# Unread matmuls in the last attention layer: extending the filler rule of a four-layer attention kernel to its final layer

## The chip, the cores and the metric

The kernel runs on one core of a Trainium2 chip. The core has a matrix engine (TensorE, PE in the profile; its weight loads are shown apart as PEld), a vector engine (VectorE, DVE), a scalar engine (ScalarE, ACT), a general engine (GpSimd, POOL) and a queue engine that issues transfers (SyncE, SP). Matmul results land in PSUM, a memory of 8 banks of 512 float columns by 128 partitions. The metric is the device time of one execution in microseconds (us), taken as the median of several runs. The profile also reports the share of its full clock that TensorE was granted, in 3.4 us steps; in this trace it is always 1.00 or 0.50.

## The reference

Four attention layers act on x of 2048 rows by 640. Each is x = x + attention(layernorm(x)) @ wo, with 32 heads of 20 columns. Layers 0 and 2 look back over a window of 256 rows; layers 1 and 3 let every query see every key (there is no causal mask).

```python
qkv = (x @ wqkv).reshape(B, S, 3, H, Dh)           # H = 32, Dh = 20
scores = einsum("bhqd,bhkd->bhqk", q, k) * Dh ** -0.5
# layers 0 and 2 only: scores = where(0 <= i - j < 256, scores, -1e9)
p = softmax(scores)
o = einsum("bhqk,bhkd->bhqd", p, v)
x = x + o.reshape(B, S, D) @ wo
```

## The kernel before

**Units, banks and tiles.** The work is cut into units (layer l, chunk c of 512 query rows, group g of four heads). A unit has one bank of scores for each pair of key block (128 keys) and head: a matmul with 32 rows (20 used) and 512 columns, four heads in four row groups of the array. Banks are handled in tiles of three, sometimes four: the score matmuls of a tile (L1308) fill PSUM banks 0 to 2 (even tiles) or 3 to 6 (odd tiles), one ACT instruction takes the exponential of the whole tile to SBUF (L1339), and some tiles later the value matmuls (L1373) multiply it with the values, which carry a column of ones, so that each head gives 21 rows. These sum up in bank 7. Scores of tile t wait until ACT has read tile t-2.

**Order.** The order of instructions on each engine is written out by the program as it runs through the tiles. Per tile: the owed unread matmuls (L1302, see below), the scores, the exponential, then `pump` (a budget of other work), `keep_clock`, value matmuls of an earlier tile, a step of the side work on VectorE, and masks for windowed layers. Other work is held in generators (tasks) that yield what they cost: layernorm, projections (L364, L465), output projections (L552, `t_out`; L584 for a part of the last one), and tails (`t_tail`), which scale a finished unit by its sums: four or eight tiny matmuls with `sel4` (L1043), a reciprocal (L1048), a transpose (L1060), a copy (L1064), four matmuls with `spread4` (L1081), a product (L1085). From layer 1 on, tasks have a single bank, number 6, for their results (`take_m`, `drop_m`), which an odd four-bank tile also uses.

**The final layer.** Its units with c = 0 are woven into earlier work. Units (3,1,0) to (3,3,7) follow with no other unit between them, from about 1611 us on; `index[3, 1, 0, None]` is the first one's place. The tasks in this stretch are the tails, the output projections of layer 3 and the part of the last one. In these units the last key block of all four heads is not given to ACT: VectorE computes its exponential by a polynomial (L910 to L941, from scores made by L903 in bank 6), and L1382 multiplies it with the values.

**Unread matmuls.** A matmul of the identity with a mask, 128 rows by 128 columns by 512, is put in where TensorE has little to do; nothing reads its result. `state["heat"]` counts full-size matmuls of a tile, `state["least"]` says how many a tile should have, `state["carry"]` brings over a surplus of at most 3, and `state["floor"]` is a least for each tile by itself. While a tile has too few (`cool`), `keep_clock` first advances a task that may run, and otherwise emits an unread matmul: by `unread` (L634) to bank 6 if that is free, or as one owed (L1302), which goes to the first bank of the next tile, ahead of its scores. `warm_bank` does the same in tails. With `least` at 0.0 none of these emit anything. `fill` (L1030) emits a fixed number in the tail of the very last unit.

## Time and profile before

| | us |
|---|---|
| median of 8 runs | 2284.76 (2281.76 to 2287.79) |
| the profiled execution | 2288.22 |
| its span, first to last instruction | 2286.5 |
| PE busy | 1982.6 (87%) |
| ACT busy | 2170.3 (95%) |
| DVE busy | 1271.8 (56%) |
| POOL busy | 271.0 (12%) |
| mean granted TensorE clock | 0.861 |

The profile page gives busy time by engine, and the span in 40 slices of 57 us, in which a digit is the busy share in tenths (9 is 90% or more) and the row PEclk is the granted clock in tenths. Other views are answers of the trace for a stretch of time: busy times by stretch, the waits of an engine with what ended them (total us, times, longest us), and the timeline, whose lines give start, duration, engine, line, result and operands, a count, and in brackets the idle time before and what ended it. The durations of matmuls are modelled and overlap; the time from one start to the next is what a matmul takes of the engine. An ACT row can begin before the one ahead has ended.

### The profile page before, as it was taken

How to read it: one execution, taken by the hardware profiler on the slowest of the kernel's cores; microseconds unless marked ns; L12 is line 12 of the kernel's file. 1: busy time of each engine (PE TensorE's matmuls, PEld its weight loads, DVE VectorE, ACT ScalarE, POOL GpSimd, SP SyncE). 2: the span in 40 equal slices, each digit the busy share in tenths (PEclk: the TensorE clock that was granted, in tenths of full speed). 3: DMA queues.
4: the chain of work that ended last, by engine and by line, in shares of the span. 5: the costliest groups of instructions: out<-in, count | busy, mean ns of one | idle time of the engine just before them, and what ended most of it. 6: DMA issues, size and time to landing. Idle time of an engine off the chain costs nothing.

```text
span 2286.5 us, 40030 instructions
## 1 busy us (share of the span) xinstructions
PE 1982.6 (87%) x15586; PEld 705.4 (31%) x15746; DVE 1271.8 (56%) x2214; ACT 2170.3 (95%) x1741; POOL 271.0 (12%) x445
## 2 busy tenths in 40 slices
PE   8899999989898998888888988898878888888887
PEld 3333343333233333233332333232221122112222
DVE  6767675435454566455564644432565565666662
ACT  7789899999999989999899999999999999999997
POOL 4322313201100122001210022011000000000000
PEclk9999999999999999999999999999755565556556
DMA  6223222322210233002320043112111111111100
GB/s 193 79 75 98 81 80 89 97 75 58 67 33 14 60 93 97 14 27 62 100 75 14 16 116 95 28 43 72 57 47 30 30 39 33 30 38 41 36 17 15
DMA packets 88284, 135.16 MB, mean 59 GB/s; under 512 B 20766, under 2 KB 63486, under 8 KB 88094
## 3 DMA queue, kind: packets, MB, share of 16 engines
q1 hardware_dynamic: 68878, 79.43, 12.6%
q0 software_dynamic: 19216, 53.17, 7.8%
q8 instruction: 123, 2.02, 0.4%
q14 instruction: 67, 0.55, 0.1%
HBM read 99.52 MB, written 27.79 MB: 56 GB/s over the span
## 4 chain that ended last, share of the span: by engine, by line
ACT 45%; PE 29%; issue 16%; DVE 9%; DMA 0%; SPq 0%; ACTq 0%; POOL 0%; DVEq 0%; POOLq 0%
ACT pt L1339 43%; PE ps L1308 7%; PE ps L364 6%; PE ps L552 5%; PE ps L1373 4%; PE ps L465 3%; DVE pt L1410 2%; PE ps L634 2%; DVE st L314 1%; DVE on L1085 1%; ACT ka L1339 1%; PE ps L1081 1%; DVE x_sb L561 1%; PE ps L429 0%; DVE raw_o L910 0%
## 5 line engine op out<-in xcount | busy, mean ns | idle before, releaser
L1339 ACT ACTIVATE pt<-ps 128x1536 bf16<-128x1536 f32 (+2 forms) x1638 | 2096.6, 1478 | 78.7 <-PE ps L1308 69.7
L1308 PE MATMUL ps<-qt,kt 32*128 32x512 bf16 x4008 | 637.6, 453 | 176.3 <-ACT pt L1339 143.2
L1373 PE MATMUL ps<-pt,vt 128*21 128x512 bf16 x3852 | 463.2, 452 | 7.1 <-issue 4.5
L1308 PEld LDWEIGHTS <-kt 32*128 32x128 bf16 x4008 | 186.2, 94 | 594.4 <-issue 575.5
L1410 DVE TENSOR_TENSOR pt<-pt,masks 128x1024 bf16<-128x1024 bf16 (+6 forms) x403 | 209.3, 553 | 151.1 <-ACT pt L1339 150.7
L634 PE MATMUL ps<-masks,ident 128*128 128x512 bf16 x708 | 244.4, 388 | 27.9 <-DVE on L1085 7.1
L364 PE MATMUL ps<-xnT,wqk 128*128 128x512 bf16 x761 | 208.2, 385 | 19.1 <-DVE on L1085 3.9
L1373 PEld LDWEIGHTS <-vt 128*21 128x21 bf16 x3960 | 99.9, 90 | 339.0 <-issue 326.8
L314 DVE CAST st<-ps 128x512 bf16<-128x512 f32 x134 | 92.6, 691 | 187.1 <-PE ps L364 177.1
L552 PE MATMUL ps<-wop,on 128*128 128x320 bf16 x928 | 163.4, 314 | 8.3 <-DVE x_sb L561 5.2
L910 DVE TENSOR_SCALAR xnT<-ps 128x512 int32<-128x512 f32 x88 | 60.8, 691 | 186.3 <-PE ps L903 186.3
L1308 PE MATMUL ps<-qa,ka 32*128 32x384 bf16 (+2 forms) x1408 | 118.5, 278 | 28.0 <-ACT pt L1339 22.6
L1085 DVE TENSOR_TENSOR on<-on,ps 128x512 bf16<-128x512 bf16 x128 | 86.3, 684 | 65.8 <-PE ps L1081 64.7
L561 DVE TENSOR_TENSOR x_sb<-x_sb,ps 128x320 bf16<-128x320 bf16 x120 | 58.0, 483 | 113.0 <-PE ps L552 112.9
L857 DVE CAST on<-ps 128x512 bf16<-128x512 f32 x112 | 77.1, 688 | 74.9 <-PE ps L1373 48.0
L465 PE MATMUL ps<-wv,xnT 128*128 128x320 bf16 x640 | 111.7, 303 | 7.9 <-DVE on L1085 3.1
L552 PEld LDWEIGHTS <-on 128*128 128x128 bf16 x928 | 83.4, 101 | 76.2 <-issue 47.6
L364 PEld LDWEIGHTS <-wqk 128*128 128x128 bf16 x830 | 70.2, 98 | 112.0 <-issue 55.7
L634 PEld LDWEIGHTS <-ident 128*128 128x128 bf16 x798 | 59.8, 97 | 132.7 <-issue 131.4
L398 POOL TENSOR_SCALAR rstd<-mv 128x4 f32<-128x4 f32 x15 | 4.1, 277 | 774.4 <-DVE mv L385 753.6
L1373 PE MATMUL ps<-pt,va 128*21 128x384 bf16 (+2 forms) x1408 | 76.2, 284 | 3.9 <-DVE pt L1410 1.6
L1308 PEld LDWEIGHTS <-ka 32*128 32x128 bf16 x1408 | 43.2, 92 | 96.3 <-issue 86.4
(101 smaller groups left out, 1585.1 us busy)
## 6 DMA issues: line engine op xcount, KB each, us to landing
vt<-v_d SPq DMA_DIRECT2D x48, 336.0 KB
kt<-k_d SPq DMA_DIRECT2D x192, 80.0 KB
wqk<-in_B_wqkv_dram POOLq DMA_DIRECT2D x80, 160.0 KB, 3.6
wqk<-in_A_wqkv_dram POOLq DMA_DIRECT2D x70, 160.0 KB, 3.4
k_d<-st POOLq DMA_DIRECT2D x75, 128.0 KB, 2.2
q_d<-st POOLq DMA_DIRECT2D x75, 128.0 KB, 2.2
qt<-q_d SPq DMA_DIRECT2D x384, 20.0 KB
v_d<-vs POOLq DMA_DIRECT2D x16, 336.0 KB, 3.0
```

The source lines that it names most:

```text
L314: nc.vector.tensor_copy(out=out_, in_=in_)
L364: nc.tensor.matmul(pq, lhsT=wt[:, dc, :], rhs=xt[:, dc, :], start=(dc == 0), stop=(dc == KD - 1),)
L465: nc.tensor.matmul(pv, lhsT=xt[:, dc, i * P : (i + 1) * P], rhs=wv_sb[l % 2][:, dc, h * HD : (h + 1) * HD], start=(dc == 0), stop=(dc == K ...
L552: nc.tensor.matmul(yp, lhsT=on[:, g, qb * P : (qb + 1) * P], rhs=wop[:, g, i * HD : (i + 1) * HD], start=(g == a), stop=(g == b - 1),)
L561: nc.vector.tensor_tensor(out=xv, in0=had, in1=yp, op=ALU.add)
L634: nc.tensor.matmul(ps[:, b, :], lhsT=ident[:], rhs=masks[:, 0, :], start=True, stop=True)
L857: nc.vector.tensor_copy(out=oT, in_=op)
L1085: nc.vector.tensor_tensor(out=oT, in0=oT, in1=zb, op=ALU.mult)
L1308: nc.tensor.matmul(sp[:, i, col * P : (col + qn) * P], lhsT=u.k(kc, j), rhs=u.q(j, q0, qn), start=True, stop=True,)
L1339: nc.scalar.activation(out=pt[:, i:k, b0 * P :], in_=sp[:, i:k, b0 * P :], func=ACT.Exp, scale=SCALE,)
L1373: nc.tensor.matmul(op[32 * j : 32 * j + VW, q0 * P : (q0 + qn) * P], lhsT=u.v(kc, j), rhs=pg[:, i, col * P : (col + qn) * P], start=(first ...
L1410: nc.vector.tensor_tensor(out=pt_[:, i:k, cols], in0=pt_[:, i:k, cols], in1=mv_, op=ALU.mult)
```

## The change

In the kernel before, `least` is 0.0 from unit (3,1,0) on. In the changed kernel it is 1.76 for a three-bank tile (2.35 for a four-bank one) there too, as in the units before; `floor` was 0.9 already. So `keep_clock` and `warm_bank` act in the final layer as they do in layers 1 and 2: they emit unread matmuls, and `keep_clock` may advance tasks. No other line differs.

```diff
                 for i, b in enumerate(cur):
                     pts.append((t, pt, i, b))
-                warmth = 1.76 if state["unit"] >= woven else 1.0
-                state["least"] = warmth * n_b / 3 if state["unit"] < index[3, 1, 0, None] else 0.0
+                state["least"] = (1.76 if state["unit"] >= woven else 1.0) * n_b / 3
                 state["floor"] = 0.9 if state["unit"] >= index[1, 1, 0, None] else 0.0
```

## The prediction

> **What bounds the kernel now.** I read the forty slices first, because they show stages. The last ten slices (from about 1611 us on) are the final layer.

> ```profile
> PE   8899999989898998888888988898878888888887
> ACT  7789899999999989999899999999999999999997
> PEclk9999999999999999999999999999755565556556
> ```

> No stage but this one runs at about half the TensorE clock, though TensorE counts as busy there, and ScalarE (ACT, the exponentials) is at 9 all the way. Next come busy times by stretch: a stretch of layers 1 and 2 with unread matmuls in it, the final layer to its last exponential, and two short stretches of half clock in earlier layers.

> ```profile
> core 0: us, PE busy (x) PEld busy (x) DVE busy (x) ACT busy (x) POOL busy (x), PEclk, DMA share, GB/s
> 600.00:800.00 200.00, 178.87 (x1449) 65.74 (x1465) 105.88 (x192) 198.14 (x172) 9.04 (x13) 1.00 0.13 35
> ...
> 1611.00:2273.00 662.00, 545.19 (x3456) 145.90 (x3456) 386.60 (x485) 649.22 (x474) 0.00 (x0) 0.55 0.11 33
> ...
> 580.00:583.40 3.40, 2.96 (x11) 0.64 (x11) 1.19 (x2) 2.90 (x2) 0.00 (x0) 0.50 0.20 50
> ...
> 842.80:846.20 3.40, 3.40 (x13) 0.79 (x12) 0.56 (x2) 1.81 (x2) 0.00 (x0) 0.50 0.28 84
> ```

> In the final layer ACT is busy 649.2 of 662 us: it is the bound, and all that a faster TensorE can give back before the last exponential is the missing 12.8 us. ACT's own waits in that stretch say who owns them:

> ```profile
> ACT pt L1339 <- PE ps L1308: 10.8, 15, 1.6
> ACT pt L1339 <- PE ps L903: 1.7, 1, 1.7
> ```

> That is 12.5 us in 16 waits, all for scores. The timeline shows what such a wait looks like at half clock:

> ```profile
> 1649.70 2.31 PE L552 MATMUL ps<-wop,on 128*128 128x320 bf16 x8
> 1651.94 0.61 PE L1373 MATMUL ps<-pt,vt 128*21 128x512 bf16 x4
> ...
> 1652.48 0.61 PE L1308 MATMUL ps<-qt,kt 32*128 32x512 bf16 x3
> ...
> 1653.20 2.79 ACT L1339 ACTIVATE pt<-ps 128x1536 bf16<-128x1536 f32 x2 [1.41 <-PE ps L1308]
> ```

> Eight output matmuls take 2.24 us from start to the next start, so the next scores come 1.41 us late. At full clock the same group takes 1.19 us (1638.32 to 1639.51). Between output projections ACT runs one three-bank tile every 1.345 us at either clock (75 tiles in 100.85 us at 1.00 from 1400 on; score matmuls 1.34 us apart at 0.50 from 1722.71 on), so there the clock buys nothing.

> **The change part by part.** Compared instruction by instruction, the program gains 747 matmuls of 128x512, each with its weight load: 303 by L634 (798 to 1101) and 444 by L1302 (70 to 514, in 268 groups of one to three, ahead of a tile's scores). All stand from the first tile of unit (3,1,0) on. Tasks move by a tile or so (output matmuls now also go 2+6), three more four-bank tiles appear for four three-bank ones, and ACT's elements and POOL's queue stay as they are. On SP one output write of c = 0 (L567) now stands ahead of the nine loads of one unit (L771 to L785) instead of behind them. It waits for its output matmuls, and the loads behind it: at most from 1644.6, where they were issued, to about 1658, the end of the fourth group of eight. A unit of 60 banks lasts 60/3 x 1.345 = 27 us and the loads are issued at the end of a unit's scores with one more unit loaded, so I cost this at nothing; without that cover it would be up to 13 us.

> *Does it hold the clock?* From 600 to 800 us there were 158 + 16 unread matmuls, and 112 + 25 real ones of 320 columns and 20 of 128; in units of 128x512 that is 174 + 86 + 5 = 265 per 200 us, at 1.00. The final layer gets 747 + 148 x 0.625 + 32 x 0.6 = 859 in 662 us, 259 per 200 us. So nearly the same, and I take 1.00. [...] The row says 0.55 at 82% busy, so it is the size of the matmuls (32 rows for scores, 21 columns for values) that fails to hold it here, and I go by the row.

> *What the fillers cost TensorE.* Start-to-start at full clock, from the stretch after 1400 us:

> ```profile
> 1421.33 0.40 PE L1308 MATMUL ps<-qt,kt 32*128 32x512 bf16 x3
> 1421.66 0.39 PE L634 MATMUL ps<-masks,ident 128*128 128x512 bf16 x1
> 1421.98 0.40 PE L1373 MATMUL ps<-pt,vt 128*21 128x512 bf16 x4
> 1422.67 0.39 PE L1308 MATMUL ps<-qt,kt 32*128 32x512 bf16 x3 [0.30 <-ACT pt L1339]
> ...
> 1424.02 0.38 PE L1302 MATMUL ps<-masks,ident 128*128 128x512 bf16 x1
> ...
> 1426.14 0.59 PE L634 MATMUL ps<-masks,ident 128*128 128x512 bf16 x2 [0.39 <-DVE on L1085]
> 1426.66 0.40 PE L1373 MATMUL ps<-pt,vt 128*21 128x512 bf16 x4
> ```

> Scores 0.33, a first unread matmul 0.32, two 0.52, values 0.33; L1302 takes 0.31 before its scores (1424.33). A usual tile (two unread, scores, values) is 0.52 + 0.33 + 0.33 = 1.18 us, under ACT's 1.345. For the whole stretch: 478 score groups x 0.33, 370 value groups x 0.33, 747 fillers x 0.27 (half first, half second) = 202, output matmuls 148 x 0.15 + 32 x 0.16, 88 side matmuls x 0.28, fourteen tails x 1.1: 158 + 122 + 202 + 27 + 25 + 15 = 549 of 662 us, 83%. It fits on the average.

> *Tile by tile* it is tight. Two L1302 in front start 0.05 after ACT frees the banks, scores follow at 0.57, ACT can start 0.50 after the scores' start (2242.76 to 2243.26), so at 1.07; ACT's own pace asks for about 1.25. Spare: 0.18 us. Three in front (six times) are 0.04 late: 0.3 us in all. A pair of tiles with a side matmul (L903) needs 1.46 + 1.18 = 2.64 of 2.69. Two tiles of a tail with fillers (0.33 + 0.32 + 0.32 + 0.33, then 0.31 more) need 2.91 of 2.69, and a filler on bank 6 waits for VectorE to read it, as at 1426.14 (0.39 us); behind that filler stand the values and the next scores, and ACT waits for these. Some 0.2 us for each of 14 tails is 3 us, and output matmuls of c = 0 (1.19 + 0.66 against 1.345) lose 1 to 2. From both sides: nothing if the slack takes it all, and 12 us if each of the 28 scalings stalls by 0.39. Nearest row: 600 to 800 us has fillers, side work, tails and outputs together and leaves ACT idle 200 - 198.14 = 1.86 us; times 662/200 it is 6.2 us. I take 6.2.

> *Dips of the clock* remain: with fillers on, the two stretches above fell to 0.50 for one window of 3.4 us and came back. ACT's waits around them sum to 0.17 + 0.35 + 0.97 = 1.5 and 0.36 + 0.59 + 1.60 = 2.6 us. None occurs from 850 to 1611 us. I take half of one, 1 us; bounds 0 and 5 dips (10 us).

> *After the last exponential* (2273.8 to 2286.5):

> ```profile
> 2275.34 1.44 PE L1030 MATMUL ps<-masks,ident 128*128 128x512 bf16 x3
> ...
> 2276.71 0.29 PE L1060 MATMUL ps<-ident,hl 128*32 128x128 bf16 x1
> ```

> Three fillers at half clock hold the transpose to 2276.71, though its operand was written by 2276.26. At full clock they take 0.32 + 2 x 0.21 = 0.74 (1.37 now), with one more by warm_bank 0.95: the transpose starts 0.4 earlier, the one filler after it saves 0.2, four L1081 0.54 to 0.32 another 0.2, the next three fillers 0.4. With the last values 0.1 to 0.2: -1.3 us. Bounds: 0 and -2.

> **Sum**, against the profiled execution's span 2286.5: -12.5 + 6.2 + 1.0 - 1.3 = -6.6, span 2279.9. That run took 2288.22, 3.5 over the median of eight, so from the median 2284.76 - 6.6 = 2278.2 us. [...]

> **Rivals.** Measurement tells 0.2% (4.6 us) from no change.
> 1. *TensorE's order becomes the wait* (slower side). Place: fillers ahead of scores (268 groups) and ahead of tails. For it: 0.18 us of spare and 2.91 against 2.69. Against: 600 to 800 us. It decides once it costs ACT over 12.5 + 1.3 + 4.6 = 18.4 us, 69 ns for each of the 268 groups, that is if a tile's matmuls take some 10% more than above. At 8 to 12%, with 14 to 20 us of new waits, 2285 to 2291.
> 2. *The clock dips often.* Tail tiles carry one filler instead of two. Each dip 1.5 to 2.6 us: six to twelve give 2284 to 2301. Against: none in 750 us before the final layer.
> 3. *The clock is not held at all*, and 747 fillers at 0.43 to 0.60 us come to 388 on top of 545: 933 against 662, +270 us, about 2555. Against: nearly equal filler rates.
> 4. *Nothing moves:* the output projections' waits stay because VectorE's reading of bank 6 paces them, or old and new waits cancel: 2281 to 2288. Against: the waits vanish at full clock (four of L584 per tile after 2243.3 leave no ACT wait).

> **How the numbers follow.** Forecast 0.55 (own range 2271 to 2282: all waits gone at one end, five us more at the other); of it 0.48 is faster by more than 0.2%, 0.07 within. Rival 1 0.20 (0.08 within, 0.12 slower), rival 2 0.15 (0.01 and 0.14), rival 3 0.04 slower, rival 4 0.06 within. Faster 0.48, same 0.22, slower 0.30. The range 2270 to 2293 leaves out rival 3, half of rival 2 and a little at either end.

> **What would show it.** Right: slices 30 to 39 of the clock at 9; ACT idle from 1611 to its last exponential 5 to 9 us, its waits behind L1302, L634 and tails rather than L552; L634 and L1302 at 0.38 us each; last exponential to end about 11.4. Wrong: clock below 0.95 there, or ACT's waits on L1308 above 14 us.

## The result, and the profile after

| | before | after |
|---|---|---|
| median, us | 2284.57 (28 runs, 2280.09 to 2290.01) | 2278.34 (10 runs, 2273.17 to 2281.59) |
| ratio, 95% interval | | 0.997 (0.9962 to 0.9978) |
| the profiled execution, us | 2288.22 | 2279.84 |
| its span, us | 2286.5 | 2278.1 |
| mean granted clock | 0.861 | 0.988 |

The changed kernel is 0.3% faster, 6.2 us by the medians; 2278.2 us was predicted. The total is right. Its parts are not all right, and two errors of the parts cancel in part; that is what most of the following is about.

The forty slices of the page of the changed kernel, tenths of busy time and of the clock:

```profile
PE   8899999989888898889888898898888888888887
ACT  7789899999999989999899999999999999999998
PEclk9999999989999999999999999999999999999999
```

The clock row was 5 and 6 in slices 30 to 39 and is 9 now. PE's row hardly differs: TensorE was counted busy before and is counted busy now. Busy times by stretch, an earlier stretch and the final layer to its last exponential:

```profile
core 0: us, PE busy (x) PEld busy (x) DVE busy (x) ACT busy (x) POOL busy (x), PEclk, DMA share, GB/s
600.00:800.00 200.00, 178.87 (x1450) 65.39 (x1468) 105.95 (x195) 197.96 (x172) 9.16 (x14) 1.00 0.14 37
...
1611.00:2266.00 655.00, 553.29 (x4146) 173.89 (x4210) 386.81 (x486) 649.84 (x474) 0.00 (x0) 0.99 0.12 33
```

The earlier stretch is as it was. In the final layer ACT has the same work (649.84 us, 649.22 before) in 655 us where it took 662, and leaves 5.2 us idle where it left 12.8. ACT's waits in that stretch (total us, times, longest us):

```profile
ACT pt L1339 <- PE ps L1308: 4.9, 10, 1.0
```

They were 12.5 us in 16 waits. And some of TensorE's waits in the same stretch:

```profile
PE ps L1302 <- ACT pt L1339: 53.1, 114, 0.9
...
PE ps L634 <- DVE on L1085: 1.3, 5, 0.4
```

The fillers (the added unread matmuls) ahead of scores wait for ACT to free their bank, 53 us in all, so for the most part it is not ACT that waits for them. A filler on bank 6 waits for VectorE's product (L1085) in only 5 places, 1.3 us in sum.

After the last exponential (timeline; start, duration, count at the end of the line):

```profile
2268.64 0.81 PE L1030 MATMUL ps<-masks,ident 128*128 128x512 bf16 x3
2269.28 0.38 PE L634 MATMUL ps<-masks,ident 128*128 128x512 bf16 x1
2269.61 0.23 PE L1060 MATMUL ps<-ident,hl 128*32 128x128 bf16 x1
```

The three fillers of L1030 and the added one of L634 now take 0.97 us up to the transpose (2268.64 to 2269.61); three alone took 1.37.

For all that follows, one measure takes out the layers ahead: the *final stretch* runs from the first four-bank exponential of the final layer to the end of the last exponential. Before it is 662.35 us, after 654.30: 8.05 less. From there to the end of the span it was 12.74 and is 10.85: 1.9 less. The final layer started 1.6 us later, though its instructions up to there are the same; in the runs of these kernels with unchanged earlier layers that start lies anywhere from 1606 to 1614 us. So -8.05 - 1.9 + 1.6 = -8.4, the difference of the two spans. Each trace is one execution: the final layer and the tail give 9.9 us here, the medians 6.2.

### The profile page after: what moved, and what is told of

It is laid out like the page before. It is cut to its first block, busy times and chain, and to the rows that moved or that the text cites. A ratio compares the mean times of both kernels' runs of the same rounds, so it can differ in the third digit from the quotient of the medians.

```text
span 2278.1 us, 41458 instructions
## 1 busy us (share of the span) xinstructions
PE 1991.6 (87%) x16267; PEld 731.7 (32%) x16493; DVE 1271.7 (56%) x2214; ACT 2169.9 (95%) x1740; POOL 271.0 (12%) x445
## 4 chain that ended last, share of the span: by engine, by line
ACT 46%; PE 28%; issue 16%; DVE 9%; DMA 0%; ACTq 0%; SPq 0%; POOL 0%; DVEq 0%; POOLq 0%
ACT pt L1339 44%; PE ps L1308 7%; PE ps L364 6%; PE ps L1372 4%; PE ps L552 4%; PE ps L465 3%; PE ps L634 2%; DVE pt L1409 2%; ACT ka L1339 2%; DVE st L314 1%; DVE on L1085 1%; PE ps L1302 1%; DVE x_sb L561 1%; PE ps L1081 1%; PE ps L429 0%
## 5 line engine op out<-in xcount | busy, mean ns | idle before, releaser
L1339 ACT ACTIVATE pt<-ps 128x1536 bf16<-128x1536 f32 (+2 forms) x1634 | 2089.1, 1448 | 71.8 <-PE ps L1308 64.2
L1308 PE MATMUL ps<-qt,kt 32*128 32x512 bf16 x4008 | 547.9, 386 | 72.5 <-ACT pt L1339 55.0
L1372 PE MATMUL ps<-pt,vt 128*21 128x512 bf16 x3840 | 395.9, 389 | 8.5 <-issue 4.5
L634 PE MATMUL ps<-masks,ident 128*128 128x512 bf16 x982 | 338.6, 390 | 33.0 <-DVE on L1085 8.4
L1308 PEld LDWEIGHTS <-kt 32*128 32x128 bf16 x4008 | 160.9, 91 | 450.8 <-issue 433.7
L1302 PE MATMUL ps<-masks,ident 128*128 128x512 bf16 x476 | 160.1, 384 | 80.9 <-ACT pt L1339 55.6
L552 PE MATMUL ps<-wop,on 128*128 128x320 bf16 x928 | 155.0, 301 | 10.3 <-DVE x_sb L561 7.3
L1308 PE MATMUL ps<-qa,ka 32*128 32x384 bf16 (+2 forms) x1408 | 117.8, 277 | 27.7 <-ACT pt L1339 22.3
L634 PEld LDWEIGHTS <-ident 128*128 128x128 bf16 x1101 | 81.4, 97 | 180.6 <-issue 178.1
L1085 DVE TENSOR_TENSOR on<-on,ps 128x512 bf16<-128x512 bf16 x128 | 86.3, 684 | 67.5 <-PE ps L1081 66.2
L552 PEld LDWEIGHTS <-on 128*128 128x128 bf16 x928 | 80.2, 97 | 71.7 <-issue 47.7
L1302 PEld LDWEIGHTS <-ident 128*128 128x128 bf16 x514 | 47.6, 96 | 137.2 <-issue 131.9
```

What stands on the lines that cost most here:

```text
L552: nc.tensor.matmul(yp, lhsT=on[:, g, qb * P : (qb + 1) * P], rhs=wop[:, g, i * HD : (i + 1) * HD], start=(g == a), stop=(g == b - 1),)
L634: nc.tensor.matmul(ps[:, b, :], lhsT=ident[:], rhs=masks[:, 0, :], start=True, stop=True)
L1085: nc.vector.tensor_tensor(out=oT, in0=oT, in1=zb, op=ALU.mult)
L1302: nc.tensor.matmul(sp[:, 0, :], lhsT=ident[:], rhs=masks[:, 0, :], start=True, stop=True)
L1308: nc.tensor.matmul(sp[:, i, col * P : (col + qn) * P], lhsT=u.k(kc, j), rhs=u.q(j, q0, qn), start=True, stop=True,)
L1339: nc.scalar.activation(out=pt[:, i:k, b0 * P :], in_=sp[:, i:k, b0 * P :], func=ACT.Exp, scale=SCALE,)
```

## The experiments

The theory: the held clock takes away ACT's waits behind output projections and shortens the tail; in the tiles between, it is worth nothing. The rival: the clock is worth something in every tile, or the gain comes from something other than the clock. For each run, waits of ACT are all its idle time between the instructions of its final stretch, short gaps too (the views of waits leave out those up to 0.15 us, so their sums are smaller), and "by dips" are those in or right behind a stretch of half clock. Each row is one traced execution.

| kernel | final stretch | to the end | ACT waits | by dips | half clock, us |
|---|---|---|---|---|---|
| before | 662.35 | 12.74 | 12.8 | 12.8 | 598 |
| after | 654.30 | 10.85 | 5.2 | 4.5 | 17 |
| e_near | 656.63 | 10.87 | 7.1 | 6.4 | 365 |
| e_far | 664.53 | 12.26 | 14.1 | 13.9 | 254 |
| e_last | 661.72 | 10.87 | 12.2 | 12.2 | 570 |
| e_nocarry | 652.46 | 10.86 | 2.8 | 0 | 0 |
| e_narrow | 657.76 | 10.88 | 8.3 | 7.8 | 31 |
| e_half | 712.34 | 10.86 | 47.0 | 47.0 | 423 |
| e_rows | 816.84 | 11.1 | 134.3 | 134.1 | 735 |
| e_w30 | 690.87 | 10.83 | 20.8 | 0 | 0 |
| e_w10nc | 686.64 | 11.9 | 28.1 | 27.9 | 229 |
| e_owed | 653.55 | 10.87 | 4.8 | 4.1 | 14 |
| e_owed_nocarry | 650.69 | 10.87 | 1.8 | 0 | 0 |

All edits are made to the changed kernel, and nothing of the computation is left out in any of them.

**Where the gain lies: fillers only near output projections and the end (e_near), or everywhere else (e_far).** e_near keeps 289 of the 747 added fillers, in the units g = 0 to 2 of each chunk, where the projections of the chunk before run, and in the last two units; e_far has fillers in the other units only (446), with the condition turned round.

```diff
                 state["least"] = (1.76 if state["unit"] >= woven else 1.0) * n_b / 3
+                v = units[state["unit"]]
+                if state["unit"] >= index[3, 1, 0, None] and not (v.g <= 2 or (v.c == 3 and v.g >= 6)):
+                    state["least"] = 0.0
```

Expected of e_near:

> Fillers in the final layer only where output projections fall: units with g 0 to 2 of each chunk, and g 6 and 7 of the last chunk (289 added fillers of 747). Theory (the gain is ACT's waits behind output projections at half clock, and the last tail): the same gain as the full change, 2277 to 2280 us, ratio 0.9965 to 0.998, though the clock stands at 0.50 between the projections. Rival (a held clock is worth something in every tile): less than half of the gain, 2281 us or more.

Expected of e_far:

> The complement: fillers only in the other units of the final layer (446 added fillers), none near the output projections and in the last two units. Theory: no gain, ACT's 12.5 us of waits stay, 2283 to 2286 us, although the clock is held over more than half of the final layer. Rival (a held clock is worth something in every tile): 2281 us or less. If fillers cost ACT time by standing ahead of scores, it shows here as a loss: over 2287 us.

e_near: 2280.08 against 2286.23 us, ratio 0.9971 (0.996 to 0.9981). e_far: 2289.94 against the same, 1.0017 (1.0009 to 1.0025). By stretch, e_near:

```profile
1611.00:2268.00 657.00, 545.75 (x3716) 152.43 (x3742) 386.51 (x485) 649.86 (x473) 0.00 (x0) 0.72 0.12 33
```

and e_far:

```profile
1611.00:2276.00 665.00, 551.09 (x3863) 165.49 (x3903) 386.56 (x485) 650.89 (x474) 0.00 (x0) 0.81 0.12 33
```

with these waits of its ACT in that stretch:

```profile
ACT pt L1339 <- PE ps L1308: 13.1, 16, 1.4
...
ACT ka L1339 <- PE ps L1308: 0.3, 1, 0.3
```

The kernel with the higher mean clock (0.81 against 0.72) is the slower one. With 39% of the fillers the gain by medians is that of the full change (0.9971 against 0.997); in the traces it is 5.7 of the 8.05 us of the final stretch, and all of the tail. With the 60% elsewhere the waits behind the output projections stay and nothing is gained. So the rival that a held clock is worth something in every tile falls. e_far is even a little slower than before, as its expectation allowed if fillers ahead of scores cost ACT time: where its fillers first set in, the clock is still at 0.50 (1663 to 1704 us), and ACT has waits of some 1.7 us in all at 1702, 1921, 2140 and 2144 us that are for scores behind them.

The change also moves tasks, since `keep_clock` may advance them, and no run changes their order alone. What speaks for the clock is e_half, below: it has the order and the number of fillers of the changed kernel, only shorter ones, its clock falls to half for 423 us, and practically all of its 47.0 us of waits lie in or behind that time.

**The end alone (e_last).** Fillers only in the last unit, (3,3,7), 28 of them: the condition above with `not (v.c == 3 and v.g == 7)`.

> Fillers in unit (3,3,7) alone, the last one (28 added). Theory: only the tail after the last exponential gains, 12.7 to 10.8 us as in the changed kernel, and perhaps 1 us of waits behind the last partial projection (L584): ratio 0.9985 to 0.9993, 2282.5 to 2284.5 us. Rival (the tail costs the same, its steps wait for VectorE): 2286 us, ratio 1.000.

2285.67 against 2286.03 us, 1.0 (0.9991 to 1.0008). That misses the expected ratio (0.9985 to 0.9993), and as a time it is inconclusive: 1.9 us is 0.08%, the edge of the interval. The trace shows the tail at 10.87 us where it was 12.74, as in the full change, and the final stretch all but unchanged (661.72).

**What makes the dips.** After 1611 us the changed kernel has three stretches of half clock, of 3.4, 10.2 and 3.4 us (at 1647.0, 1882.5 and 2254.6), 17 us in sum. The timeline of its ACT around two of them:

```profile
1630.18 6.82 ACT L1339 ACTIVATE pt<-ps 128x1536 bf16<-128x1536 f32 x5 [0.31 <-PE ps L1308]
1637.23 10.85 ACT L1339 ACTIVATE pt<-ps 128x1536 bf16<-128x1536 f32 x8 [0.23 <-PE ps L1308]
1648.28 1.45 ACT L1339 ACTIVATE pt<-ps 128x1536 bf16<-128x1536 f32 x1 [0.20 <-PE ps L1308]
1649.90 1.45 ACT L1339 ACTIVATE pt<-ps 128x1536 bf16<-128x1536 f32 x1 [0.17 <-PE ps L1308]
...
1886.37 1.45 ACT L1339 ACTIVATE pt<-ps 128x1536 bf16<-128x1536 f32 x1 [1.02 <-PE ps L1308]
1888.41 1.45 ACT L1339 ACTIVATE pt<-ps 128x1536 bf16<-128x1536 f32 x1 [0.60 <-PE ps L1308]
1890.88 4.40 ACT L1339 ACTIVATE pt<-ps 128x1536 bf16<-128x1536 f32 x3 [1.01 <-PE ps L1308]
```

and of its TensorE ahead of and in the first dip (1647.0 to 1650.4 us):

```profile
1635.22 1.26 PE L552 MATMUL ps<-wop,on 128*128 128x320 bf16 x8
1636.41 0.40 PE L1372 MATMUL ps<-pt,vt 128*21 128x512 bf16 x4
...
1648.10 0.61 PE L1372 MATMUL ps<-pt,vt 128*21 128x512 bf16 x4
1648.64 0.61 PE L1302 MATMUL ps<-masks,ident 128*128 128x512 bf16 x1
1649.18 0.61 PE L1308 MATMUL ps<-qt,kt 32*128 32x512 bf16 x3
1649.73 1.58 PE L552 MATMUL ps<-wop,on 128*128 128x320 bf16 x8
1651.23 0.40 PE L1372 MATMUL ps<-pt,vt 128*21 128x512 bf16 x4
```

Behind eight output matmuls at full clock (1635.22) ACT waits 0.23 us and then runs eight tiles without a wait. Behind the same eight in the dip (1649.73) it waits 0.71 us. Of 5.2 us of waits, 4.5 belong to the dips. Busy times by stretch for the 3.4 us ahead of each dip (first, third and last row), and of a stretch that was followed by full clock though it has no more fillers (second row):

```profile
1643.60:1647.00 3.40, 2.15 (x14) 0.60 (x14) 1.52 (x3) 3.40 (x4) 0.00 (x0) 1.00 0.56 153
...
1868.90:1872.30 3.40, 2.89 (x25) 0.71 (x21) 1.19 (x3) 3.40 (x4) 0.00 (x0) 1.00 0.14 48
1879.10:1882.50 3.40, 1.75 (x17) 0.58 (x14) 0.92 (x1) 3.40 (x4) 0.00 (x0) 1.00 0.00 0
...
2251.10:2254.50 3.40, 1.56 (x12) 0.48 (x9) 0.00 (x0) 3.40 (x3) 0.00 (x0) 1.00 0.00 0
```

Of the filler lines alone, each of the three has three weight loads of L1302 and none of L634. One filler per tile is the `floor` of 0.9: the output matmuls just ahead had counted as heat, and their surplus, carried over by up to 3.0, met `least` for the tiles that follow. Fillers are then few and so is all else (TensorE is busy 1.6 to 2.2 us of 3.4; in the second row, 2.9). e_nocarry takes the surplus away in the final layer, which adds 902 fillers in place of 747:

```diff
-        state["carry"] = min(max(spare, 0.0), 3.0)
+        most = 0.0 if state["unit"] >= index[3, 1, 0, None] else 3.0
+        state["carry"] = min(max(spare, 0.0), most)
```

> The changed kernel, but in the final layer a tile's surplus is not carried over to the next ones (carry limited to 0 there, 902 added fillers instead of 747). Theory: the three dips of the clock in the changed kernel's trace follow the output projections, where the carried surplus lets tiles go with 0.9 of a filler; without it no dip after 1611 us is left, ACT's waits fall from 4.9 to about 1 us, and the time by 3 to 4 us to 2274 to 2275. Rival (TensorE's order is already near full, 155 more fillers make ACT wait): 2279 us or more.

2275.29 against 2286.23 us, 0.9947 (0.9935 to 0.9959). By stretch:

```profile
1611.00:2264.00 653.00, 580.75 (x4289) 182.31 (x4359) 387.70 (x489) 647.60 (x472) 0.00 (x0) 1.00 0.12 33
```

and ACT's waits in it:

```profile
ACT pt L1340 <- PE ps L1309: 1.8, 7, 0.5
```

(one line was added, so L1339 is L1340 here.) No dip is left, and the gain grows from 0.3 to 0.5%. The carry makes the dips: taking it away puts 155 more fillers where the surplus had excused them. ACT keeps 2.8 us of waits (1.8 in the view; about 1 was expected), at full clock, behind output matmuls and in tiles with tails.

**Less carry in the earlier layers too (e_c1):** the same edit with 1.0 in place of 3.0 ahead of the final layer.

> No carry in the final layer and a carry of at most 1.0 instead of 3.0 in all earlier ones (1894 fillers in all; 1779 with the final layer's carry alone taken away). Theory (dips follow carried surplus): the four dips between 225 and 850 us go too, at 1.5 to 2.6 us each, 4 to 8 us below the kernel without carry in the final layer alone, 2268 to 2272 us. Rival (earlier layers have projections, and TensorE is full there): no gain over it, 2275 us or more.

2296.69 against 2286.03 us, 1.0046 (1.0034 to 1.0058): slower. Its final stretch is that of e_nocarry (652.45 us), but it starts at 1630 us instead of 1611. By stretch, e_c1:

```profile
200.00:400.00 200.00, 188.15 (x1698) 71.89 (x1697) 132.11 (x279) 174.52 (x150) 51.53 (x79) 0.97 0.29 81
```

and the kernel before:

```profile
200.00:400.00 200.00, 185.07 (x1739) 76.91 (x1756) 135.55 (x286) 185.13 (x160) 50.23 (x77) 0.98 0.27 79
```

In the first 400 us TensorE has input projections to do beside the scores, and ACT gets less done (174.5 us of 200, 185.1 before) with the clock nearly as it was. So the rival of the expectation has the time right. Its reason is not shown: the weight loads of fillers (L634) in this stretch are 53 against 45, too few for 11 us, and `keep_clock` also advances tasks earlier when a tile is short. It is the same knob, and it helps in one stage and costs in the other.

**How many fillers: too many (e_w30) and too few (e_w10nc).** e_w30 asks for 3.0 a tile in the final layer (1330 added); e_w10nc for 1.0 and no carry (462 added).

```diff
                 state["least"] = (1.76 if state["unit"] >= woven else 1.0) * n_b / 3
+                if state["unit"] >= index[3, 1, 0, None]:
+                    state["least"] = 3.0 * n_b / 3
```

> The changed kernel with 3.0 instead of 1.76 fillers for a three-bank tile in the final layer (1330 added fillers instead of 747). It measures the price of a full TensorE. By my spacing (third fillers at 0.22 us, 583 more) TensorE needs 549 + 128 = 677 us against ACT's 645: ACT waits 30 to 40 us and the time is 2305 to 2315 us, clock 0.99. Rival (the slack between score matmuls and ACT swallows more than the spacing says, as the 2 us of waits outside dips hint): below 2290 us.

> 1.0 filler for a three-bank tile in the final layer, and no carry there (462 added fillers). If what the clock needs is a level in every 3.4 us and not on the mean, an even 1.0 holds it as well as 1.76 with a carry: clock in the final layer 0.97 or more, ACT's waits 2 to 5 us, 2275 to 2278 us. Rival (1.0 is below what the clock needs): many dips, clock below 0.9 there and 2281 us or more.

e_w30: 2312.02 against 2286.03 us, 1.012 (1.0105 to 1.0135). e_w10nc: 2305.35, 1.0077 (1.0057 to 1.0097). By stretch, and the waits of ACT in it, e_w30:

```profile
1611.00:2298.00 687.00, 671.61 (x4763) 208.11 (x4766) 386.68 (x484) 666.22 (x471) 0.00 (x0) 1.00 0.11 32
```

```profile
ACT pt L1339 <- PE ps L1308: 18.6, 77, 0.4
```

and e_w10nc:

```profile
1611.00:2294.00 683.00, 582.82 (x3905) 163.16 (x3904) 385.64 (x484) 654.80 (x470) 0.00 (x0) 0.83 0.11 32
```

```profile
ACT pt L1340 <- PE ps L1309: 25.7, 72, 1.3
```

e_w30 came out as expected: TensorE is busy 672 of 687 us, and ACT has 77 short waits of at most 0.4 us in the view. The waits do not make up the whole loss. The final stretch is 36.6 us longer than in the changed kernel: 15.6 us of it are idle time, and 21 us are ACT's busy time, which grew for the same work. The timeline tells what that is:

```profile
1800.64 12.50 ACT L1339 ACTIVATE pt<-ps 128x1536 bf16<-128x1536 f32 x9 [0.39 <-PE ps L1308]
```

An exponential that starts behind a wait takes 1.45 us; one that can begin before the one ahead has ended ends 1.34 us after it, so that eight take 10.85 us in the changed kernel (1637.23). Nine at that pace would take 12.2 us; here they take 12.50. In e_w30 scores come just late enough that the overlap is lost, up to 0.1 us a tile, and the profile counts that as busy. Added up over the final stretch, the lost overlap is 22 us, and 2 in the changed kernel.

e_w10nc missed what I expected. The clock does not hold (0.83), and at half clock even one filler is too much for a tile: values, a filler and scores take 0.54 us each from start to start in the dip above (1648.10 to 1649.73), 1.6 us where ACT has room for 1.345; without the filler it would be 1.1. So too few fillers are worse than none: 28 us of waits in place of 12.8, all but 0.3 of them in or behind 229 us of half clock.

**Which fillers held the clock here.** The prediction blamed the size, rows and columns. Three runs change one size of the same fillers: 32 weight columns in place of 128 (e_narrow), 32 rows in place of 128 (e_rows), 256 moving columns in place of 512 (e_half). e_narrow:

```diff
-            ps[:, b, :], lhsT=ident[:], rhs=masks[:, 0, :], start=True, stop=True
+            ps[0:m, b, :], lhsT=ident[:, 0:m], rhs=masks[:, 0, :], start=True, stop=True
```

with m = 32 in the final layer, and alike for L1302.

> The changed kernel with fillers of 32 columns instead of 128 in the final layer: the same 747 added matmuls, rows and moving columns, a quarter of the array. Theory (the clock goes by how much of the array works, not by how long TensorE is busy): the clock falls to 0.50 for most of the final layer, the fillers cost 0.43 to 0.60 us each, and the time rises by 150 to 300 us to 2430 to 2580. Rival (busy time or the pauses decide): clock 0.98 or more and 2275 to 2285 us.

One run: 2277.09 us (2286.23 before), by stretch

```profile
1611.00:2264.00 653.00, 552.77 (x4182) 157.63 (x4180) 384.93 (x483) 644.73 (x470) 0.00 (x0) 0.98 0.12 33
```

That was against my theory of the time, the used area of the array. With a quarter of the columns the clock is at 0.98. Its 31 us of half clock, where the trace of full fillers has 17, are no shown difference: over the whole span its mean clock is 0.989, and the ten runs of the changed kernel lie from 0.988 to 0.992.

In e_rows all fillers stand ahead of scores, as in e_owed below (32-row fillers in bank 6 were not tried), and use the rows of the tile's first head:

```diff
+                    r = slice(0, P)
+                    if state["unit"] >= index[3, 1, 0, None]:
+                        r = slice(32 * cur[0][1], 32 * cur[0][1] + 32)
                     nc.tensor.matmul(
-                        sp[:, 0, :], lhsT=ident[:], rhs=masks[:, 0, :], start=True, stop=True
+                        sp[:, 0, :], lhsT=ident[r, :], rhs=masks[r, 0, :], start=True, stop=True
```

> As the kernel with all fillers ahead of scores, but each filler uses 32 rows of the array instead of 128, the row group of the tile's first head, so that it is in order with the scores of its bank. If the rows in use decide what the clock grants (scores have 32 rows too), the clock of the final layer falls to 0.5 to 0.7 and the time to above 2290 us. If only the time for which the array streams decides, the clock stays at 0.97 or more and the time at 2274 to 2282 us.

One run: 2435.9 us (2284.71 before), by stretch

```profile
1611.00:2423.00 812.00, 780.27 (x4180) 182.01 (x4180) 387.06 (x483) 677.74 (x470) 0.00 (x0) 0.55 0.09 26
```

TensorE is busy 780 of 812 us, 96%, and is granted 0.55, no more than before with no filler at all. With 128 rows in the same places the clock is 0.99 (e_owed, 1611 to 2266 us).

e_half cuts `w` from 512 to 256 in `ps[:, b, 0:w]` and `masks[:, 0, 0:w]`, and likewise ahead of scores; the count stays 747.

> The changed kernel with fillers of 256 moving columns instead of 512 in the final layer, the same 747 added. If streamed time decides, this is worth 0.88 of a filler per tile, less than the even 1.0 that left the clock at 0.50 for 229 us of the final layer: clock below 0.9 there and 2290 us or more (the shorter fillers cost less than those, so not above 2305). If the number of matmuls decides: clock 0.97 or more, 2272 to 2279 us.

One run: 2331.05 us (2284.71 before), by stretch

```profile
1611.00:2318.00 707.00, 635.38 (x4175) 179.09 (x4175) 386.62 (x483) 659.98 (x469) 0.00 (x0) 0.70 0.11 30
```

As many fillers with half the length do not hold it here: 0.70, against 0.99 with 512 columns. So their count alone does not tell the clock; fewer rows (e_rows) and fewer moving columns both lowered it in this stretch. The loss is larger than I had bounded it (at most 2305).

**Where the fillers stand (e_owed, e_owed_nocarry).** All fillers of the final layer ahead of a tile's scores (L1302), none to bank 6 (L634): 745 in all.

```diff
-        if cool() and (
+        if state["unit"] < index[3, 1, 0, None] and cool() and (
             state["credit"] <= 0.0 or all(task.wake > state["tick"] for task in todo)
...
-            if mfree[b][0] > state["tick"] - (0 if state["early"] else 0):
+            if state["unit"] >= index[3, 1, 0, None] or mfree[b][0] > state["tick"]:
                 state["owed"] += 1
```

> The changed kernel with all fillers of the final layer placed ahead of scores (745 by L1302, none by L634, so none writes bank 6 and none waits for VectorE). It tests the two places of waits that I priced at 6.2 us. If waits for bank 6 cost ACT time, this is 1 to 3 us faster than the changed kernel, 2275 to 2277 us. If the place ahead of the scores costs it (two fillers leave 0.18 us of spare, three none), it is slower, 2281 us or more. If neither, as ACT's 0.7 us of waits outside dips say, 2277 to 2280 us, and what differs are the dips.

2274.11 against 2284.71 us, 0.9962 (0.9951 to 0.9974), 20 runs from 2270.84 to 2291.07. That is 10.6 us under the kernel before, where the full change is 6.2 under it, but the intervals overlap. Whether fillers on bank 6 cost a few us is not settled: without carry the same edit differs the same way (14.2 us against 10.9, next run), while the traced final stretches differ by 0.75 and 1.8 us only. With 745 instead of 444 fillers in front of scores, ACT waits no longer (4.8 us, 4.1 of it by dips).

e_owed_nocarry has both edits.

> Both edits that were faster than the changed kernel: all fillers of the final layer ahead of scores, and no carry there. If dips were what was left, taking away the carry removes them in this form too, and the waits for bank 6 are already gone: 2272 to 2275 us, no half clock after 1611 us, ACT's waits there below 3 us. Rival (902 fillers all ahead of scores are often three to a tile, which is late by 0.04 us or more each time): above 2276 us.

2271.74 against 2285.97 us, **0.9941 (0.9928 to 0.9955)**: the fastest kernel of the study, 14.2 us under the kernel before. By stretch, with the waits of ACT:

```profile
1611.00:2260.00 649.00, 574.47 (x4273) 183.98 (x4348) 386.03 (x485) 645.65 (x471) 0.00 (x0) 1.00 0.11 34
```

```profile
ACT pt L1340 <- PE ps L1309: 1.2, 5, 0.3
ACT pt L1340 <- ACT pt L1340: 0.3, 1, 0.3
```

The final stretch is 11.7 us shorter than before and the tail 1.9, in sum 13.5: nearly all of the 12.5 us of waits and 1.3 us of tail that stand in the prediction's sum.

## Why the prediction was right, and where its steps were not

- *What bounds the kernel.* Right. ACT's work did not change, and the gain of the final stretch came out of its 12.8 us of idle time. With ACT busy 649.2 of 662 us, 98%, the best kernel still gained 0.6%, by way of what ACT waited for.
- *Does it hold the clock?* Right on the mean, 0.99. The clause on why was half wrong. 32-row fillers fail (0.55) as the clause has it, but 32-column fillers hold (0.98), so few columns are not what fails; for the 21 columns of the value matmuls themselves no run shows it. And the equal mean rate, 259 against 265 per 200 us, did not mean an equal clock throughout: 17 us of the final layer were at half clock. The 0.55 of the kernel before came with TensorE 82% busy and a longest wait of its matmuls of 1.2 us, the 0.55 of e_rows with TensorE 96% busy.
- *The 12.5 us of waits behind output projections.* Right in the main. At full clock such a wait, up to 1.7 us before, shrinks to 0.2 or 0.3, and e_near and e_far show that the gain lies there and in the tail. In the changed kernel eight output matmuls take 1.19 us from start to start (1635.22 to 1636.41), as was read off the trace of before.
- *New waits with fillers, 6.2 us.* This step failed. Outside the dips ACT waits 0.7 us in the changed kernel, and 0.31 and 0.23 of it (1630.18 and 1637.23) are behind output matmuls, not behind L1302, L634 or tails. It was scaled from the stretch of 600 to 800 us of the kernel before, whose 1.86 us of idle time I put down to fillers, tails and bank 6. Its ACT has six waits there, and these three, 0.7 us in all, are behind output matmuls too:

```profile
728.67 58.93 ACT L1339 ACTIVATE pt<-ps 128x1536 bf16<-128x1536 f32 x45 [0.26 <-PE ps L1308]
787.83 10.43 ACT L1339 ACTIVATE pt<-ps 128x1536 bf16<-128x1536 f32 x8 [0.23 <-PE ps L1308]
798.45 2.79 ACT L1339 ACTIVATE pt<-ps 128x1536 bf16<-128x1536 f32 x2 [0.20 <-PE ps L1308]
```

  The other three, 1.2 us, fall in two of its seven tails. So scaling that row by time counted output waits as new ones, and counted them too high: the stretch has 112 output matmuls in 200 us, the final layer 148 + 32 in 662. The tile-by-tile sum beside it (0.18 us of spare) was closer: it gave no waits for a usual tile. The 2.91 against 2.69 us of tail tiles and the 0.39 us at bank 6 (now five waits) hardly reach ACT.
- *Dips, 1.0 us.* This step was mis-sized: three dips and 4.5 us. "None from 850 to 1611 us" did not carry over, since output projections with their surplus, and then tiles in which TensorE has little to do, come in this order in the final layer. The cause stood in the code (`carry` up to 3, `floor` 0.9) and e_nocarry shows it (no half clock).
- *The tail, -1.3 us.* -1.9, in its bounds.
- *The sum.* The predicted waits were 12.5 - 6.2 - 1.0 = 5.3 us less; measured are 12.8 - 5.2 = 7.6 less: one step took 5.5 us of new waits too many, the other 3.5 us of dips too few. With the 1.6 us by which this run's final layer began late, the span fell by 8.4, and the median by 6.2, where 6.6 was forecast. That the median came within 0.2 us is luck: the errors offset each other in part, and the rest is the spread of some 8 us between runs.
- *SP's write ahead of nine loads.* Costed at nothing, and nothing shows: all of ACT's waits in the final layer are for scores behind TensorE, and none of TensorE's is for a transfer.
- *Rival 1* (TensorE's order becomes the wait) is real but further off than its 8 to 12%: it decides in e_w30, with 1330 fillers. *Rival 2* (dips) is what costs the change most, though with three dips in the traced run and not six. (Six to twelve dips at 1.5 to 2.6 us, on top of 2277 us, would be 2286 to 2308, not the 2284 to 2301 that it gave.) *Rival 3* (clock not held) is told by e_rows, +151 us; the +270 of the prediction is for full-row fillers at half clock, which no run has. *Rival 4* fell: most of the waits did go.

## What to carry to other kernels

In this kernel unread matmuls are worth placing where the engine that bounds it waits for TensorE, and not elsewhere; ask for the waits, not for the mean clock. Look at the fillers in stretches as short as the dips, and not only at their mean rate: at a mean clock of 0.99 the changed kernel still had three dips, ahead of which TensorE was busy 1.6 to 2.2 us of 3.4, and 4.5 of ACT's 5.2 us of waits belong to them. So in the final layer no surplus should be carried into tiles with little work, while in the first 400 us carrying less cost time (e_c1, 1.0046). Here too few fillers were worse than none (e_w10nc, 1.0077), and too many filled TensorE (e_w30, 672 of 687 us). When ACT comes late by less than its overlap, the loss is counted as busy time, so compare the length of a stretch and not only its waits. When a forecast rests on a wait scaled from another stretch, first look at what that stretch's waits are for.
